# A new order of steps in a fused recurrence and MLP kernel on one core: two more key chunks turned by DMA, fillers placed anew

## The chip, the cores and the metric

The kernel runs on one core of one Trainium2 chip. The metric is the device time of one execution in microseconds (us). The engines of the core are TensorE (PE in the profile, PEld for its weight loads), VectorE (DVE), ScalarE (ACT), GpSimd (POOL) and SyncE (SP). SP computes nothing: it issues DMAs.

## The reference

Two stages, in float32. The first is a linear recurrence with decay over 768 steps, for 4 batches and 8 heads of 48 columns; the second is a normalised MLP with a residual, over the 384 columns of all heads together.

```python
for t in range(S):                                  # S = 768
    cur = u * k_t (outer) v_t
    y[:, :, t] = r_t @ (state + cur)
    state = w[..., None] * state + k_t (outer) v_t
x = y.transpose(0, 2, 1, 3).reshape(B, S, H * D)    # 4 x 768 x 384
xn = (x - mean(x)) / sqrt(var(x) + 1e-6) * g_ln
out = x + relu(xn @ w_ch1) @ w_ch2                  # 384 -> 1536 -> 384
```

## The kernel before

The 768 steps of a batch are cut into 6 chunks of 128 rows, so there are 24 chunks, numbered through all batches. Within a chunk the recurrence is done as masked attention with decay factors multiplied into r and k; from chunk to chunk of a batch a state Z (48 x 48 for each head) is carried. The MLP runs over groups of chunks (`GROUPS`: eight of one chunk, six of two, four of one).

The kernel is a list of small steps, worked out by a planner and written out in the string `PLAN`. A step `NAME,i,e` stands for the function of that name called with number i and engine e (v DVE, s ACT, g POOL, - where the engine is fixed). The steps are issued in the order of the list, and each engine runs its own in that order: a step that waits holds all that is behind it on its engine, and SP's DMAs are held in the same way. The list is what sets the order; nothing is rescheduled later.

The steps, by line of the profile:

- Loads on SP: LK (L344), LR (L349 for two chunks together, L354 for one), LV (L357) bring k, r, v of a chunk; LW1 (L327) a third of the first MLP matrix. IW2 (L341) brings a third of the second matrix on POOL's queue.
- SK and SR (L208) multiply k and r by decay factors; CV (L203, L205) copies v to bf16. The buffers of k, r and v hold 10 chunks.
- Turns: TRK, TRR (L382) turn keys or the queries of two chunks on PE, and TCk, TCr (L203 on ACT, L205 on DVE) copy them out of PSUM. For the chunks of `K_BY_DMA` the keys are turned by DMA instead: TKD (L546) from chunk 12, with the queries still on PE, and TKR (L540) from chunk 14, both together.
- Q (L208) multiplies turned r and k. AT (L414) makes the scores on PE, AM, or AMa and AMb for half of it, (L424) masks them on DVE.
- S (L445, L452, L458) makes the next state and the diagonal term on PE; ZU (L208 or L471) and ZD (L208) update Z; CC (L203, L205) copies the diagonal term; VB (L477) multiplies it with v.
- Y (L487, L495) makes the chunk's output on PE, X (L502) adds VB on DVE, SQ (L509), RS (L523, L526) and XN (L515, L517) normalise.
- The normalised chunk is turned on PE (LT, L555, with copy XT) or by DMA (LT2, L534, for two chunks; LTD, L530).
- UP (L570) is a part of the first matrix product, RL (L586 on ACT, L588 on DVE) its relu, DN (L599) a third of the second product of a chunk. `UP,i` is part i mod 16 of group i div 16, `DN,i` third i mod 4 of chunk i div 4. OT (L657) adds the residual; STO (L664) and STP (L668) store one or two chunks, on ACT's queue (s) or SP's (-). The last chunk goes in halves: DA, DB (L616), OA, OB (L632), SA, SB (L645).
- SW (L334, L338) scales a block of the first matrix; WBM (L298), FK (L302), FR (L306), WL (L320), CT (L231) and CP make factors at the start.
- WU and DU (L281, L285) are matmuls of zeros whose results nobody reads. As long as no DN has been issued a DU,8 is two matmuls of 512 columns into a PSUM tile of its own; afterwards it is eight matmuls of 128 columns into the unread columns of the latest `o` tile.

PSUM has one tile each for `at`, `s`, `y`, `tr` and `o`, and two for `hp`. So the next AT waits for AM, the next Y for X, the next chunk's DN for OT, and so on.

Of the kernel before, what the change touches and what calls it, by code (L numbers as in the profile page):

```python
# [26 lines left out]
SW,3,s X,1,v SW,7,g TRK,3,- S,2,- AM,2,v LV,4,- TCk,3,s XN,1,g UP,0,- CC,2,s SW,8,s LT,1,- VB,2,v Y,2,- SW,6,s
LK,6,- XT,1,v AT,3,- Q,3,v RL,0,s UP,1,- X,2,v SK,4,g CV,3,s UP,17,- ZU,2,v XN,2,s RL,1,v S,3,- SQ,0,s LT,2,-
DU,8,- CC,3,v RL,17,s XT,2,v VB,3,g DU,8,- SQ,2,s TRK,4,- IW2,2,g SR,4,v UP,33,- TCk,4,s SR,5,v RS,0,g UP,34,- RL,33,s
AM,3,v LR,6,- TRR,4,- RS,2,g RL,34,s UP,18,- LV,6,- TCr,4,v Q,4,v DN,0,- RL,18,s ZU,3,v LV,5,- UP,32,- TCr,5,s SK,5,v  # L30
AT,4,- RL,32,s Y,3,- CV,4,g UP,2,- X,3,v TRK,5,- AM,4,v XN,3,g RL,2,s DN,1,- TCk,5,s S,4,- LK,7,- UP,16,- Q,5,v
CC,4,v SK,6,v LT,3,- LK,8,- DN,2,- VB,4,g XT,3,v UP,48,- LR,8,- SR,7,g OT,0,v TRK,6,- ZU,4,v DN,8,- LV,7,- TCk,6,s
SR,6,g Y,4,- RL,16,s LV,10,- DN,9,- X,4,v TRR,6,- XN,4,g DN,10,- TCr,7,v TCr,6,s SK,7,g AT,5,- RL,48,s OT,2,v S,5,-
UP,49,- LK,12,- CC,5,s CV,6,s AM,5,v SQ,1,s DN,4,- LR,10,- CV,5,s TRK,7,- RL,49,v RS,1,g DN,5,- TCk,7,s LK,11,- Q,6,v
AT,6,- SQ,3,s SR,8,v Y,5,- LK,9,- VB,5,v LT,4,- S,6,- XT,4,s SK,8,g UP,50,- X,5,v CC,6,v AM,6,v DN,6,- XN,5,s
LV,8,- Q,7,g CV,7,s UP,64,- LR,12,- RL,50,s OT,1,v Y,6,- SR,9,g SQ,5,s AT,7,- ZU,6,v LV,9,- LT,5,- RL,64,s UP,66,-
XT,5,v VB,6,g AM,7,v CV,10,s LK,10,- TRK,8,- S,7,- TCk,8,s UP,81,- RL,66,s CC,7,v ZU,7,v DN,12,- VB,7,g STO,1,s X,6,v
SQ,4,s TRR,8,- RS,5,g XN,6,v DN,13,- LR,14,- RL,81,s TCr,9,v SK,9,g TCr,8,s UP,82,- LV,12,- Y,7,- RS,3,g LT,6,- LV,15,-
AT,8,- X,7,v XT,6,s DN,14,- Q,8,g SQ,6,s TRK,9,- RL,82,s UP,65,- LR,15,- RS,4,g SR,12,v XN,7,s UP,98,- TCk,9,v RL,65,s
LR,16,- SR,11,g OT,3,v CV,8,s LT,7,- STO,3,s LV,13,- UP,80,- ZD,7,v STO,0,s AM,8,v SR,10,g DN,16,- RL,80,s S,8,- RL,98,s  # L40
SK,10,g DN,17,- XT,7,v LK,13,- CC,8,v ZU,8,v Y,8,- CV,9,g TRR,10,- LK,14,- DN,18,- Q,9,v TCr,11,s SK,11,v AT,9,- TCr,10,s
OT,4,v VB,8,g UP,112,- LV,11,- AM,9,v ZD,8,g TRK,10,- DN,20,- X,8,v S,9,- STO,2,- DN,21,- CC,9,s SK,12,v TCk,10,s Y,9,-
VB,9,g ZU,9,v SQ,8,s TKD,12,- UP,96,- RL,112,s RS,6,g Q,10,v TRK,11,- X,9,v RL,96,s AT,10,- ZD,9,g DN,22,- AM,10,v XN,9,s
UP,113,- XN,8,s SR,14,g TCk,11,s OT,5,v UP,97,- LT2,8,- SR,13,v S,10,- RL,97,s DN,24,- Q,11,v CV,12,s LR,17,- ZU,10,v SK,13,g
AT,11,- CC,10,s CV,11,s RL,113,v DN,25,- LK,15,- VB,10,g AM,11,v S,11,- TKD,13,- TRR,12,- DN,26,- TCr,12,s SR,15,g CC,11,v Y,10,-
SQ,7,s LK,16,- UP,130,- ZD,10,v STO,4,- Q,12,g X,10,v UP,132,- RL,130,s LK,18,- OT,6,v Y,11,- RL,132,s LV,14,- UP,114,- RS,7,g
VB,11,v TCr,13,v DN,28,- X,11,v AT,12,- SK,14,v XN,11,s UP,128,- SR,16,v TKR,14,- RL,114,s AM,12,v S,12,- SQ,10,s DN,29,- SK,15,g
XN,10,s UP,129,- ZU,12,v RL,128,s CV,13,g TKR,15,- DN,30,- RL,129,s Q,13,v Y,12,- SQ,9,s AT,13,- OT,7,v UP,131,- SQ,11,s LT2,10,-
AM,13,v UP,133,- CC,12,s RL,131,s DN,32,- CV,14,s VB,12,v STO,7,- RL,133,s S,13,- LV,17,- AT,14,- CC,13,v X,12,v DN,33,- VB,13,g
LR,18,- ZU,13,v Y,13,- LK,17,- RS,8,g Q,15,v DN,34,- Q,14,v UP,147,- SK,16,g LR,19,- OT,8,v S,14,- AM,14,v RL,147,s DN,36,-  # L50
CV,15,g TKR,16,- UP,144,- RS,9,g ZD,13,v AT,15,- X,13,v RL,144,s UP,146,- CC,14,v ZU,14,v XN,13,s UP,145,- VB,14,v STO,5,s XN,12,v
DN,37,- STO,6,s RL,145,v LT2,12,- SQ,12,s Y,14,- AM,15,v S,15,- RL,146,s DN,38,- SK,18,g LV,16,- UP,148,- OT,9,v LK,21,- SR,17,g
UP,149,- RL,148,s DN,40,- SK,17,v RL,149,s AT,16,- ZD,14,v TKR,17,- DN,41,- X,14,v SR,18,g ZU,15,v UP,160,- CC,15,v Q,16,v LV,18,-
Y,15,- VB,15,g AM,16,v RL,160,s DN,42,- LK,19,- SQ,13,s CV,16,g UP,163,- TKR,18,- OT,10,v CV,17,g UP,165,- RL,163,s ZD,15,v RS,10,g
DN,44,- XN,14,s X,15,v RL,165,s UP,162,- XN,15,v UP,161,- Q,17,v LT2,14,- RL,162,v DN,45,- RL,161,s CV,18,v S,16,- SQ,15,s LV,19,-
DN,46,- SK,19,v LR,21,- AT,17,- Q,18,g OT,11,v UP,164,- ZU,16,v STP,10,- DN,48,- RL,164,s CC,16,v SR,19,v S,17,- STP,8,s ZD,16,g
AM,17,v Y,16,- DN,49,- TKR,19,- UP,181,- VB,16,v DN,50,- X,16,v SR,21,g LR,20,- SQ,16,s AT,18,- LK,20,- UP,177,- OT,12,v CC,17,s
SQ,14,s AM,18,v LV,21,- Y,17,- RL,181,s DN,52,- RL,177,s VB,17,v S,18,- DN,53,- CC,18,s SK,21,g CV,19,s X,17,v UP,178,- VB,18,v
UP,176,- RL,178,s XN,16,v Y,18,- XN,17,v AT,19,- RL,176,s Q,19,v LT2,16,- DN,54,- SR,20,v UP,180,- OT,13,v UP,179,- LR,23,- X,18,v
ZU,18,v TKR,21,- DN,56,- RL,179,s SK,20,v S,19,- RL,180,s XN,18,v DN,57,- CC,19,v SQ,17,s AM,19,v LV,20,- UP,193,- RS,12,g TKR,20,-  # L60
UP,197,- VB,19,v RL,193,s RS,11,g Y,19,- RL,197,s UP,196,- LR,22,- X,19,v DN,58,- XN,19,v RL,196,s LT2,18,- UP,192,- OT,14,v UP,194,-
ZU,19,v RL,192,s CV,20,v LK,22,- DN,60,- SR,23,v RL,194,s STP,12,- Q,20,v AT,20,- ZD,19,g DN,61,- AM,20,v LK,23,- S,20,- DN,62,-
SR,22,g ZU,20,v UP,195,- OT,15,v Q,21,g UP,213,- RL,195,s DN,64,- ZD,20,v RL,213,s CV,21,v Y,20,- CC,20,s SK,22,v DN,65,- VB,20,g
TKR,22,- UP,209,- X,20,v S,21,- SK,23,g DN,66,- RL,209,v XN,20,s UP,208,- CC,21,v LTD,20,- OT,16,v AT,21,- RL,208,s DN,68,- AM,21,v
STP,14,s LV,22,- UP,211,- Q,22,g SQ,20,s LV,23,- DN,69,- RL,211,v TKR,23,- UP,210,- VB,21,v ZU,21,v DN,70,- Y,21,- OT,17,v UP,212,-
CV,22,s RL,210,v DN,72,- RL,212,s X,21,v S,22,- SQ,18,s ZD,21,v DN,73,- CC,22,s ZU,22,v SQ,19,s UP,225,- XN,21,v RS,13,g VB,22,v
DN,74,- LTD,21,- UP,226,- Q,23,g OT,18,v AT,22,- RL,225,v RL,226,s DN,76,- RS,14,g AM,22,v STP,16,s UP,224,- ZD,22,g DN,77,- RL,224,s
Y,22,- SQ,21,s DN,78,- X,22,v RS,15,g S,23,- UP,241,- SQ,22,s OT,19,v XN,22,g AT,23,- CC,23,s DN,80,- CV,23,g AM,23,v LTD,22,-
UP,240,- RS,16,g VB,23,v DN,81,- RL,240,s Y,23,- RL,241,s DN,82,- STP,18,s X,23,v UP,256,- XN,23,s OT,20,v UP,242,- LTD,23,- RL,256,v
# [641 lines left out]
```

## Time and profile before

| | us |
|---|---|
| median of 3 runs | 154.26 (152.65 to 155.15) |
| profiled execution | 153.76 |
| its span, first to last instruction | 151.9 |
| PE busy | 142.9 (94%) |
| DVE busy | 116.9 (77%) |
| ACT busy | 81.1 (53%) |
| POOL busy | 80.6 (53%) |

The page gives busy times of the engines, the span in 40 slices, the DMA queues, a chain of waits followed back from the end, and groups of instructions by line. Matmuls are pipelined, so a busy PE may still be waiting; the starts of its instructions tell more than the busy share. The granted PE clock was full in all slices.

### The profile page before, as it was taken

Reading aid. Unit: us, or ns where it says so; the run is one execution under the profiler, and the core shown is the slowest. Engines: PE = TensorE matmul, PEld = TensorE weight load, DVE = VectorE, ACT = ScalarE, POOL = GpSimd, SP = SyncE. Lnnn points to the kernel's source line nnn. Section 1 sums busy time; section 2 is a strip of 40 time slices with the busy share of each in tenths; the row PEclk is TensorE's granted clock in tenths of the full one; section 3 lists DMA queues with packets and bytes.
Section 4 is the critical chain, followed back from the end, with each engine's and each line's share of the span. In section 5 each row is a group of like instructions: output and inputs, shape, how many; then the busy total and the mean of one; then the engine's idle time right before and its main releaser. Section 6 shows DMA issues by size and latency. Waiting matters only on the chain.

```text
span 151.9 us, 4412 instructions
## 1 busy us (share of the span) xinstructions
PE 142.9 (94%) x1774; PEld 109.3 (72%) x1774; DVE 116.9 (77%) x237; ACT 81.1 (53%) x181; POOL 80.6 (53%) x122
## 2 busy tenths in 40 slices
PE   7999679999999999999999999999998999999991
...
DMA  5999979999999996399989898995995493325021
GB/s 122 229 246 339 340 154 216 224 220 218 223 233 234 190 261 159 84 154 191 184 178 239 182 174 137 309 172 108 193 199 165 94 228 56 129 43 169 0 107 53
DMA packets 90900, 27.16 MB, mean 179 GB/s; under 512 B 86140, under 2 KB 89344, under 8 KB 90880
## 3 DMA queue, kind: packets, MB, share of 16 engines
...
## 4 chain that ended last, share of the span: by engine, by line
PE 64%; DVE 9%; DMA 9%; POOL 6%; issue 4%; ACT 4%; SPq 2%; DVEq 0%; POOLq 0%; ACTq 0%
PE hp L570 24%; PE o L599 22%; DMA vf<-in_v_dram 7%; PE at L414 4%; PE tr L382 3%; PE o L281 3%; DVE A L424 2%; DMA xT<-xn 2%; DVE ot L657 2%; PE y L495 2%; PE s L458 2%; PE y L487 1%; POOL rs L526 1%; ACT sqj L509 1%; PE s L445 1%
## 5 line engine op out<-in xcount | busy, mean ns | idle before, releaser
L570 PE MATMUL hp<-xT,w_sb 128*128 128x128 bf16 (+1 forms) x648 | 57.0, 237 | 0.3 <-DMA xT<-xn 0.3
L599 PE MATMUL o<-w_sb,hT 128*128 128x384 bf16 x276 | 56.0, 326 | 0.7 <-DVE ot L657 0.6
L586 ACT ACTIVATE hT<-hp 128x512 bf16<-128x512 f32 x60 | 35.1, 594 | 34.5 <-PE hp L570 34.0
L570 PEld LDWEIGHTS <-w_sb 128*128 128x128 bf16 x648 | 49.4, 114 | 5.0 <-DMA xT<-xn 0.7
L599 PEld LDWEIGHTS <-hT 128*128 128x128 bf16 x276 | 24.1, 97 | 11.8 <-issue 1.0
L424 DVE TENSOR_TENSOR A<-at,mask 128x1024 bf16<-128x1024 f32 (+1 forms) x26 | 29.3, 1133 | 1.1 <-PE at L414 1.1
L657 DVE SCALAR_TENSOR_TENSOR ot<-o,rs,x 128x384 f32<-128x384 f32 x23 | 14.1, 615 | 9.9 <-PE o L599 6.1
L208 POOL TENSOR_TENSOR sc<-kf,Fk 128x384 bf16<-128x384 f32 x13 | 13.7, 1054 | 13.9 <-PE s L458 8.1
L502 DVE SCALAR_TENSOR_TENSOR x<-y,Vb 128x384 f32<-128x384 f32 x24 | 13.2, 551 | 6.3 <-PE y L495 4.1
L477 POOL TENSOR_TENSOR Vb<-vf,cc 128x384 f32<-128x384 f32 x11 | 9.7, 878 | 13.5 <-DVE cc L205 6.9
L509 ACT ACTIVATE sqj<-x,sm 128x384 bf16<-128x384 f32 x24 | 14.7, 615 | 3.6 <-DVE x L502 2.8
L203 ACT COPY trs<-tr 128x512 bf16<-128x512 bf16 x19 | 11.0, 586 | 10.6 <-PE tr L382 7.1
L281 PE MATMUL o<-warm 128*128 128x512 bf16 x49 | 13.7, 415 | 1.0 <-DVE warm L237 1.0
L523 POOL TENSOR_SCALAR rs<-sq 128x1 f32<-128x1 f32 (+1 forms) x18 | 4.6, 253 | 17.6 <-ACT sqj L509 16.5
L208 POOL TENSOR_TENSOR sc<-rf,Fr 128x384 bf16<-128x384 f32 x12 | 12.7, 1068 | 0.9 <-DMA out_dram<-ot 0.6
L526 POOL TENSOR_TENSOR rs<-rs,expo 128x1 f32<-128x1 f32 (+1 forms) x18 | 12.0, 665 | 1.5
L208 POOL TENSOR_TENSOR q<-trs 128x512 bf16<-128x512 bf16 x8 | 10.3, 1287 | 3.5 <-DMA trs<-sc 3.5
L208 DVE TENSOR_TENSOR sc<-rf,Fr 128x384 bf16<-128x384 f32 x12 | 8.2, 692 | 4.3 <-ACT Fr L306 3.8
L414 PE MATMUL at<-trs 48*128 48x128 bf16 x192 | 9.5, 219 | 1.0 <-ACT trs L203 1.0
L414 PEld LDWEIGHTS <-trs 48*128 48x128 bf16 x192 | 5.5, 94 | 6.2 <-issue 5.2
L382 PE MATMUL tr<-ident,sc 128*128 128x128 bf16 x104 | 8.9, 219 | 0.3 <-DVE trs L205 0.2
L588 DVE TENSOR_SCALAR hT<-hp 128x512 bf16<-128x512 f32 x12 | 8.2, 685 | 0.9 <-PE hp L570 0.9
...
## 6 DMA issues: line engine op xcount, KB each, us to landing
...
```

The lines of the kernel that those rows point to most:

```text
L208: engines[e].tensor_tensor(out=out, in0=in0, in1=in1, op=ALU.mult)
L281: nc.tensor.matmul(out=warm_ps[0][:], lhsT=warm[:], rhs=warm[:].unsqueeze(1).to_broadcast([P, 4, P]), start=True, stop=True)
L382: nc.tensor.transpose(out=t[:, a * HP + q, :], in_=flat[:, q, :], identity=ident[:])
L414: nc.tensor.matmul(out=t[:, par, q, :], lhsT=trs(i)[p0 : p0 + D, 1, q, :], rhs=trs(i)[p0 : p0 + D, 0, q, :], start=True, stop=True,)
L424: nc.vector.tensor_tensor(out=AA(i)[:, a:b].rearrange("p e q t -> p (e q) t"), in0=psum["at", i][:, a:b].rearrange("p e q t -> p (e q) t") ...
L502: nc.vector.scalar_tensor_tensor(out=xx(i)[:], in0=psum["y", i][:, :C], scalar=1.0, in1=Vb(i)[:], op0=ALU.mult, op1=ALU.add, accum_out=sm[ ...
L509: nc.scalar.activation(out=sqj[:], in_=xx(i)[:], func=ACT.Square, bias=sm[i][:], scale=-float(C), accum_out=sq[g][:, j : j + 1])
L526: nc.gpsimd.tensor_tensor(out=rs[g][:], in0=rs[g][:], in1=expo[:, :n], op=ALU.pow)
L570: nc.tensor.matmul(out=t[:, a * gw : (a + 1) * gw].rearrange("p (j t) -> p j t", j=size), lhsT=w1_sb[n][kc][:, fb::FB], rhs=xT(g)[:, :size ...
L586: nc.scalar.activation(out=o, in_=s, func=ACT.Relu)
L599: nc.tensor.matmul(out=psum["o", i][:, :C], lhsT=hT(g)[:, fk, j * P : (j + 1) * P], rhs=w2_sb[d][:, a, :], start=(fk == 0), stop=(fk == FK ...
L657: nc.vector.scalar_tensor_tensor(out=ot(i), in0=psum["o", i][:, :C], scalar=rs[g][:, j : j + 1], in1=xx(i)[:], op0=ALU.mult, op1=ALU.add,)
```

## The change

The list `PLAN` is another one, and the keys of chunks 10 and 11 join `K_BY_DMA`. The functions are the same. Counted over both lists (834 steps each):

| step | before | after |
|---|---|---|
| TRK, TCk | 12 each | 10 each |
| TKD | 2 | 4 |
| DU | 23, all ahead of the first DN | 24 ahead of it, 1 behind DA,2 |
| CC on ACT / DVE | 11 / 13 | 20 / 4 |
| SK on POOL / DVE | 13 / 11 | 16 / 8 |
| SR on POOL / DVE | 12 / 12 | 8 / 16 |
| Q on POOL / DVE | 8 / 16 | 6 / 18 |
| VB on POOL / DVE | 11 / 13 | 14 / 10 |
| XN on ACT / DVE / POOL | 11 / 8 / 5 | 14 / 7 / 3 |
| TCr on ACT / DVE | 8 / 6 | 12 / 2 |
| TCk on ACT / DVE | 11 / 1 | 4 / 6 |
| XT on ACT / DVE | 3 / 5 | 6 / 2 |
| RL on ACT / DVE | 60 / 12 | 61 / 11 |
| CV on ACT / DVE / POOL | 12 / 4 / 8 | 11 / 5 / 8 |
| SW on ACT / POOL | 6 / 3 | 5 / 4 |
| STO and STP on ACT / SP | 11 / 6 | 5 / 12 |

The diff, cut to the set of chunks, the start and the end of the list:

```diff
-K_BY_DMA = [12, 13, 14, 15, 16, 17, 18, 19, 20, 21, 22, 23]
+K_BY_DMA = [10, 11, 12, 13, 14, 15, 16, 17, 18, 19, 20, 21, 22, 23]
...
-MW,0,v WF,0,s MI,0,g LR,0,- MP,0,v DU,8,- LC,0,s LK,0,- TL,0,s MM,0,g DU,8,- LK,2,- WU,13,- LN,0,s LV,0,- LC,1,s
-LV,1,- WBM,0,- DU,8,- LK,1,- FR,1,s DU,8,- FK,0,s SR,0,v DU,8,- LR,2,- FR,2,s SK,0,v DU,8,- FR,0,s SR,1,v TRK,0,-
-LC,2,- DU,8,- SK,2,v TCk,0,s LK,3,- DU,8,- CV,0,s LW1,1,- TRR,0,- DU,8,- LV,2,- TCr,0,s TCr,1,v DU,8,- SK,1,g LW1,0,-
-AT,0,- AMa,0,v LW1,2,- CV,1,g TRK,1,- AMb,0,v LV,3,- CT,0,- DU,8,- Q,0,g CP,0,s TCk,1,s LK,4,- DU,8,- Y,0,- DU,8,-
-UW,0,g Q,1,v AT,1,- SR,2,v TRK,2,- SR,3,g S,0,- TCk,2,s DU,8,- LR,4,- UGC,0,s CC,0,s DU,8,- WL,0,s VB,0,g DU,8,-
-SW,5,s TRR,2,- SW,4,g CV,2,v ZU,0,v SK,3,g X,0,v S,1,- DU,8,- CC,1,v AMa,1,v DU,8,- AMb,1,v DU,8,- SW,0,s SW,1,g
-DU,8,- TCr,3,v TCr,2,s XN,0,g ZU,1,v SW,2,s IW2,1,g AT,2,- VB,1,v LT,0,- Y,1,- Q,2,v IW2,0,g XT,0,s LK,5,- DU,8,-
...
+MW,0,v WF,0,s MI,0,g LV,0,- MP,0,v WU,13,- LC,1,s LK,0,- TL,0,s LK,2,- DU,8,- LR,0,- LN,0,s DU,8,- LC,2,s LK,3,-
+DU,8,- CV,0,g WBM,0,- LK,1,- DU,8,- FK,0,s DU,8,- FR,1,s LV,1,- SK,2,v DU,8,- FR,2,s SK,0,v TRK,2,- DU,8,- LR,2,-
+TCk,2,v DU,8,- SR,1,v TRK,0,- LC,0,- SR,0,v DU,8,- TCk,0,s LW1,1,- DU,8,- LV,2,- TRR,0,- SK,1,g DU,8,- LW1,2,- TCr,0,s
+DU,8,- MM,0,g TCr,1,s LW1,0,- AT,0,- Q,0,v CV,1,s LK,4,- TRK,1,- DU,8,- SR,3,v LK,5,- CT,0,- DU,8,- TCk,1,v CP,0,s
+FR,0,s DU,8,- UW,0,g AMa,0,v WL,0,s AMb,0,v UGC,0,s SR,2,v LV,3,- AT,1,- Q,1,v S,0,- TRR,2,- AMb,1,v CC,0,s SK,3,g
+Y,0,- DU,8,- TCr,2,s AMa,1,v SW,3,s CV,2,g ZU,0,v AT,2,- VB,0,v S,1,- Q,2,v DU,8,- CC,1,s TCr,3,s X,0,v DU,8,-
+SW,5,s ZU,1,v TRK,3,- XN,0,g DU,8,- AM,2,v TCk,3,s VB,1,g Y,1,- SQ,0,s S,2,- SW,6,g LT,0,- SW,8,s X,1,v DU,8,-
+ZU,2,v SW,7,g AT,3,- XT,0,s LR,4,- Y,2,- XN,1,s AM,3,v SW,4,g DU,8,- CC,2,s LK,6,- DU,8,- RS,0,g SW,2,s VB,2,v
+LT,1,- DU,8,- SQ,1,s LV,4,- X,2,v UP,1,- SW,0,g SW,1,s DU,8,- IW2,0,g SK,4,v XT,1,s UP,0,- SK,5,v RL,1,s IW2,1,g
+XN,2,v TRK,4,- RS,1,g RL,0,s UP,17,- LV,5,- TCk,4,v CV,3,s Q,3,v TRK,5,- RL,17,s LR,6,- UP,18,- IW2,2,g TCk,5,v SR,4,v
+LT,2,- S,3,- RL,18,s LK,7,- XT,2,v Y,3,- SR,5,v CC,3,s UP,2,- ZU,3,v SK,6,g TRR,4,- RL,2,s UP,33,- VB,3,v TCr,4,s
+TCr,5,v UP,32,- RL,33,s X,3,v AT,4,- UP,16,- XN,3,v Q,4,v DN,0,- Q,5,v CV,4,v LR,8,- TRK,6,- AM,4,v S,4,- TCk,6,s
...
-RL,258,s RL,272,s DN,90,- STO,21,s UP,274,- OT,22,v DB,0,- STO,22,- RL,274,s DA,0,- DB,1,- DA,1,- DB,2,- DA,2,- OB,23,v OA,23,v
+RL,273,s RL,272,s DN,90,- DB,0,- OT,22,v UP,274,- STO,22,s DA,0,- RL,274,v DB,1,- DA,1,- DB,2,- DA,2,- OB,23,v DU,8,- OA,23,v
 SB,23,s SA,23,-
```

SP's order in the later part, where stores and turns stand among the loads:

```text
before  LK22 STP12 LK23 TKR22 LTD20 LV22 LV23 TKR23 LTD21 LTD22 LTD23 STO22 SA23
after   LK18 LR18 TKR17 LK19 LK22 STP8 LT2,14 TKR18 LK20 LV18 TKR19 LV19 LR20 LV20 LT2,16 STP10 LV21 LR21 LK21
        TKR20 STP12 LT2,18 LK23 LR22 TKR21 LV22 LR23 TKR22 STP14 TKR23 LTD20 LV23 LTD21 LTD22 LTD23 STO21 STP18 SA23
```

More of the change, by code (lines that the diff above doesn't have):

```diff
@@ L27 @@
[L27 to L69, printed above, removed]
@@ new lines @@
+UP,34,- OT,0,v UP,49,- X,4,v CV,5,s VB,5,g LV,6,- DN,8,- RL,34,s RS,2,g XN,4,s UP,50,- SR,7,v SQ,3,s LV,7,- DN,9,-
+SR,6,v SK,7,g RL,50,v LK,10,- LT,4,- Y,5,- XT,4,s DN,10,- RL,49,s SQ,4,s TRR,6,- OT,2,v UP,48,- LV,10,- TCr,7,s SR,9,g
+UP,66,- TCr,6,s LR,15,- SK,8,v DN,4,- RL,66,s X,5,v SR,8,g LK,11,- AT,6,- RL,48,s TRK,7,- AM,6,v CV,6,s DN,5,- CV,7,g
+LK,9,- XN,5,s UP,65,- RS,3,g Q,6,v LV,8,- DN,6,- TCk,7,v RL,65,s Q,7,v S,6,- LR,10,- OT,1,v AT,7,- CC,6,s LT,5,-
+VB,6,g Y,6,- DN,12,- XT,5,v LR,12,- ZU,6,v RS,4,g TRK,8,- X,6,v DN,13,- TCk,8,s AM,7,v S,7,- SQ,5,s TRR,8,- LV,12,-
```

35 lines of the change are left out of this document (34 added, 1 removed).

## The prediction

> **What bounds the kernel now.** I began with the page's first two parts, then laid the step order of PLAN beside TensorE's timeline.
>
> ```profile
> PE 142.9 (94%) x1774; PEld 109.3 (72%) x1774; DVE 116.9 (77%) x237; ACT 81.1 (53%) x181; POOL 80.6 (53%) x122
> ...
> PE   7999679999999999999999999999998999999991
> ...
> DMA  5999979999999996399989898995995493325021
> ```
>
> PE is full but for the first fifth and a few late slices, and the DMA engines are full in the first third. A busy PE may still lose time, so I need step lengths: from one step's first start to the next one's, in the PE timeline (start, us, line; idle time before in brackets).
>
> ```profile
> 20.63 0.36 PE L495 MATMUL y<-vv,A 128*128 128x48 bf16 x8
> 20.84 0.59 PE L281 MATMUL o<-warm 128*128 128x512 bf16 x2
> 21.27 0.39 PE L382 MATMUL tr<-ident,sc 128*128 128x128 bf16 x4
> 21.49 0.24 PE L445 MATMUL s<-uwI,q 128*128 128x2 bf16 x4
> 21.59 0.32 PE L452 MATMUL s<-Z,ident 128*128 128x384 bf16 x1
> 21.75 0.33 PE L458 MATMUL s<-vv,sc 128*128 128x96 bf16 x4
> 21.92 0.83 PE L570 MATMUL hp<-xT,w_sb 128*128 128x128 bf16 x12
> 22.59 0.33 PE L555 MATMUL tr<-ident,xn 128*128 128x128 bf16 x3
> 22.76 0.33 PE L487 MATMUL y<-Z,trs 128*128 128x96 bf16 x4
> 22.93 0.36 PE L495 MATMUL y<-vv,A 128*128 128x48 bf16 x8
> 23.22 0.40 PE L414 MATMUL at<-trs 48*128 48x128 bf16 x8
> 23.55 1.53 PE L570 MATMUL hp<-xT,w_sb 128*128 128x128 bf16 x24
> ```
>
> So Y is 0.38 (22.76 to 22.93, 20.63 to 20.84), an early DU 0.43, TRK 0.22, S 0.43 (0.27 without L452), UP 0.67, LT 0.17, AT 0.33, with some 0.08 more ahead of each AT (22.93 to 23.22 against 20.63 to 20.84). The chain of waits gives two more:
>
> ```profile
> 28.46 0.45 PE tr L382 x8
> ...
> 29.58 0.65 PE o L599 x4
> ```
>
> TRR is 0.45 and DN 0.65. By count: 72 UP at 0.66 (the wide ones stream the same columns) 47.7, 69 DN 44.9, 24 AT 7.9, 24 Y 8.4, 24 S 6.5, TRK, TRR and LT 7.1, six last steps 2.0, 23 DU 9.9, and about 2.9 for WU, WBM and CT: 137.3 us of **PE time** in a span of 151.9. So the order's PE work sets the time, and there remain some 10 us of starts, waits and tail, the only thing that a new order can win. Where they lie:
>
> ```profile
> 9.86 0.40 PE L414 MATMUL at<-trs 48*128 48x128 bf16 x8
> ...
> 16.64 0.24 PE L445 MATMUL s<-uwI,q 128*128 128x2 bf16 x4 [1.21 <-DVE Z L208]
> ...
> 19.95 0.40 PE L414 MATMUL at<-trs 48*128 48x128 bf16 x8 [0.99 <-ACT trs L203]
> ...
> 29.42 0.81 PE L599 MATMUL o<-w_sb,hT 128*128 128x384 bf16 x4
> ...
> 100.52 0.65 PE L599 MATMUL o<-w_sb,hT 128*128 128x384 bf16 x3 [0.34 <-DVE ot L657]
> ...
> 114.64 0.25 PE L445 MATMUL s<-uwI,q 128*128 128x2 bf16 x4 [0.87 <-DVE q L208]
> ...
> 137.53 1.53 PE L570 MATMUL hp<-xT,w_sb 128*128 128x128 bf16 x24 [0.34 <-DMA xT<-xn]
> ...
> 148.01 0.49 PE L616 MATMUL o<-w_sb,hT 128*128 128x192 bf16 x4
> ```
>
> DN,0 starts at 29.42 with 23.8 of PE time ahead of it and 113.5 behind it: 4.6 us lost ahead beside the 1.0 of the start. From 29.42 to PE's end at 148.34 (148.01 and one step of 0.33) are 118.9, so 5.4 are lost behind DN,0; about 1.9 are the 0.08 ahead of the ATs, which stay, and **3.5 are waits**.
>
> **The change part by part.** *Turns by DMA.* TRK,10 and TRK,11 go (2 x 0.22 = 0.44 off PE), with two copies; two turns come onto SP's queue. Times to landing of the two in the trace:
>
> ```profile
> DMA to landing us min/median/max: 2.5/3.6/4.6
> ```
>
> In the new order they are issued 7.4 and 9.1 us of PE time ahead of their first readers, so I cost them at nothing: PE's steps between are the cover, and without it one costs 3.6, at most 4.6, less than either lead.
>
> *Unread matmuls.* 24 early DU instead of 23: +0.43. The 25th stands behind DA,2, the last step, eight 128-column matmuls of 0.67/12 us each: 0.45. It writes unread columns of the accumulator that OA reads. Whether OA waits for it the trace of before cannot show; bounds 0 and 0.45. I take 0.45, as OA is behind it in the order and on one bank. PE time is then 137.3 - 0.44 + 0.43 + 0.45 = 137.7: **no gain in work**.
>
> *Moved work.* DVE gives up nine CC, three SK, three VB, four TCr and takes five TCk, four SR, two Q. From the groups by line (mean ns ahead of the bar's last column):
>
> ```profile
> L477 DVE TENSOR_TENSOR Vb<-vf,cc 128x384 f32<-128x384 f32 x13 | 7.7, 596 | 0.0
> L208 DVE TENSOR_TENSOR q<-trs 128x512 bf16<-128x512 bf16 x16 | 7.7, 489 | 0.4 <-ACT trs L203 0.2
> L208 DVE TENSOR_TENSOR sc<-kf,Fk 128x384 bf16<-128x384 f32 x11 | 7.5, 685 | 0.5 <-PE s L458 0.5
> ...
> L205 DVE COPY trs<-tr 128x512 bf16<-128x512 bf16 x7 | 4.5, 648 | 2.3 <-ACT trs L203 1.5 <-PE tr L382 0.8
> ...
> L205 DVE COPY cc<-s 128x8 f32<-128x8 f32 x13 | 2.1, 159 | 1.2 <-PE s L458 1.1
> ```
>
> With SR at SK's price: -1.4 - 2.1 - 1.8 + 0.65 + 2.7 + 1.0 = -0.9 us. DVE is not heavier, ACT and POOL stand at 53%; load does not decide, positions do.
>
> *The start.* In before S,1 waits for Z, because CV,2 stands ahead of ZU,0 on DVE and waits for its load:
>
> ```profile
> 15.39 0.74 DVE L205 CAST vv<-vf 128x384 bf16<-128x384 f32 x1 [1.81 <-DMA vf<-in_v_dram]
> 16.05 0.54 DVE L208 TENSOR_TENSOR Z<-s,WLZ 128x384 bf16<-128x384 f32 x1
> ...
> 17.35 1.28 DVE L424 TENSOR_TENSOR A<-at,mask 128x512 bf16<-128x512 f32 x2
> ```
>
> CV,2 goes to POOL, but DVE gets the copy of chunk 1's keys. PE's lag at AT,0 is 1.2 (9.86 less the start of 1.0 less 7.7 of PE time); with it TRK,1 ends at about 11.5 in the new order. Behind it on DVE: TCk 0.65, two half masks 1.28, SR 0.55, Q 0.42, two half masks 1.28, Z 0.54, in all 4.7, so S,1 at about 16.3 instead of 16.64. From S,1 to DN,0 the new order has 13.5 of PE time (11.1 in before: it brings real work forward). AT,2, which waited 0.99 for TCr,2 behind TCr,3 and a weight scaling, now stands ahead of S,1; its copy comes first. On this stretch I add 0.2 for two ATs and 0.5 for chunk 4's queries:
>
> ```profile
> 26.93 1.02 DVE L208 TENSOR_TENSOR sc<-rf,Fr 128x384 bf16<-128x384 f32 x2 [0.50 <-DMA rf<-in_r_dram]
> ...
> 15.86 3.75 SPq L349 DMA_DIRECT2D rf<-in_r_dram  x1
> ```
>
> LR,4, issued at 15.86, landed only near 26.9. The new order puts LK,5 ahead of it, but issues the second matrix's loads (19.0 in before, row below) behind SW,0, which follows RS,0 and so SQ,0 on ACT: at about 22.6, an estimate from the orders and the page's durations. So LR,4 meets less of them. SR,4 can start at 25.3 by DVE's order. Bounds: no wait (LR,4 at 25), or 2.7 (at 28.0, 26.9 and one load more). I take 0.5, nearer to the first, as the competing loads start later. Those loads then land in time for DN,0:
>
> ```profile
> L341 POOL DMA_DIRECT2D w_sb<-in_moe_w_ch_dram x3: 543/607/786, 19.0 to 27.0; - x3
> ...
> DMA to landing us min/median/max: 5.5/6.3/6.8
> ```
>
> that is 28.1 to 29.4. **DN,0 at 16.3 + 13.5 + 0.7 = 30.5**, with 111.2 left: 141.7, against 29.42 + 113.5 = 142.9. **Gain 1.2**, the last DU paid.
>
> *Behind DN,0.* I set, for every ring of one or two PSUM tiles and each chain such as Y, X, XN, turn, UP, the PE time between releasing and waiting step against the durations: none of either order is too short by more than 0.1 us, so the 3.5 come from engines that run late. Of the largest, LV,22 no longer stands behind two waiting turns and LTD,22 has 3.7 of PE time to its UP instead of 2.3; LTD,20 is tighter (2.4 instead of 6.2). I keep 2.5 of the 3.5: **gain 1.0**, bounds 3.0 (only 0.5 stays) and a loss of 3.3 (below).
>
> Sum: 153.76 (the profiled execution, 1.9 above its span) - 2.2 = 151.6; against the median 154.26 it is **152.1 us**, and I forecast on that scale. A measurement of this kernel tells about 2% from no change, 3.1 us.
>
> **Rivals.** *A, the waits nearly all go:* LR,4 in time and no AT late gains 1.9 ahead of DN,0, 3.0 behind: 154.26 - 4.9 = 149.4. For it: all slacks are positive. Against: before's are too, and it still lost 8 us.
>
> *B, SP's line holds the loads.* SP takes six more stores and two turns. STP,8, waiting for OT,9, now stands ahead of LT2,14, TKR,18, LK,20 and LV,18; CV,18 on ACT needs LV,18 3.6 of PE time after its issue. Rows of before for such a hold (SP waits, then ACT waits):
>
> ```profile
> SPq L540 <- DVE sc L208: 5.5, 4, 3.4
> ...
> ACT vv L203 <- DMA vf<-in_v_dram: 3.3, 1, 3.3
> ```
>
> It decides once DVE runs more than STP,8's lead of 4.9 us late; then XN,16, RL,179 and S,18 queue behind CV,18. One hold of 3.3 on PE with before's late waits kept: 154.26 - 1.2 + 3.3 = 156.4, slower; two make 159.7. Against it: the other stores stand 3.6 us and more behind their OT. The Trainium skill, page "DMA: Bandwidth & Descriptors", section "Anatomy of one DMA — SWDGE (gpsimd) path", says that DMA engines never wait on semaphores and the issuing sequencer does, which speaks against a store on SP; the trace's waits of SP agree.
>
> *C, the early loads stay the bound:* LR,4 lands at 28.0, DVE stands 2.7 at SR,4, TRR,4 and all behind follow, DN,0 at 32.7: 0.8 to 1.0 lost there, 1.0 gained later: 154.2, no change. For it: DMA slices of 9 until 60 us. That the change does nothing is part of this case.
>
> **How the numbers follow.** Forecast 0.45 (own range 150.7 to 153.5), A 0.22, B 0.15, C 0.18. Range 149.3 to 156.8: it takes in A, C and one hold of B, and leaves out two holds. Faster by over 2% (below 151.2): A and a quarter of the forecast, 0.33. Slower by over 2% (above 157.3): two holds or one of C on top, 0.13. Within 2%: 0.54.
>
> **What would show it.** S,1 near 16.3 and its wait for Z gone; DN,0 at 30 to 31; the wait before L208's first two-row group of chunk 4 below 1 us; PE's last step 0.45 longer; behind DN,0 about 2.5 us of waits, none above 1. Wrong if DN,0 is past 31.7, if ACT waits 3 us for a value load, or if the waits behind DN,0 are above 4 us in sum.

## The result, and the profile after

The changed kernel took 153.11 us (median of 20 runs, 150.43 to 155.49), the kernel before 154.20 us on the same chip (20 runs, 152.65 to 156.85). The ratio is 0.986 with a 95% interval of 0.982 to 0.990: faster by 1.4%, clear of no change, but by less than 2%. Every ratio here leaves out the executions that ran over 1.5% longer than the fastest of their kernel, which are 12 of these 20 of the changed kernel, its first profiled one among them; the medians of all 20 give 0.993. Two further measurements gave 0.984 (0.979 to 0.989) and 0.986 (0.981 to 0.990). The rows below are from the second profile of the changed kernel, an execution of 152.21 us; the first, of 153.54 us, and the third, of 150.77 us, are used for the scatter.

The page of the changed kernel:

```profile
span 150.4 us, 4424 instructions
...
PE 143.3 (95%) x1776; PEld 109.6 (73%) x1776; DVE 114.4 (76%) x225; ACT 81.9 (54%) x192; POOL 78.8 (52%) x121
...
PE   7999999999999999999998999999999998999991
...
DMA  5999999999979988999999898996998964312321
```

TensorE's share rose by a point because the span shrank, not its work. The first fifth of its row is filled, and the DMA engines, which had a gap in slices 16 and 17 before (6 and 3), now stand at 6 or more until slice 33, but for the first.

TensorE's timeline of the changed kernel, at the places that the prediction named (start, us, line; idle time before in brackets):

```profile
16.14 0.24 PE L445 MATMUL s<-uwI,q 128*128 128x2 bf16 x4
...
22.47 0.59 PE L281 MATMUL o<-warm 128*128 128x512 bf16 x2
23.43 0.86 PE L570 MATMUL hp<-xT,w_sb 128*128 128x128 bf16 x12 [0.37 <-POOL w_sb L338]
...
30.50 0.81 PE L599 MATMUL o<-w_sb,hT 128*128 128x384 bf16 x4
...
32.22 0.81 PE L599 MATMUL o<-w_sb,hT 128*128 128x384 bf16 x4 [0.25 <-DMA w_sb<-in_moe_w_ch_dram]
...
34.30 0.81 PE L599 MATMUL o<-w_sb,hT 128*128 128x384 bf16 x4 [0.22 <-DMA w_sb<-in_moe_w_ch_dram]
...
67.94 0.23 PE L414 MATMUL at<-trs 48*128 48x128 bf16 x2 [0.46 <-DMA trs<-sc]
...
127.06 0.86 PE L570 MATMUL hp<-xT,w_sb 128*128 128x128 bf16 x12 [0.51 <-DMA xT<-xn]
...
146.46 0.61 PE L291 MATMUL o<-warm 128*128 128x128 bf16 x8
```

S,1 (16.14) no longer waits, and DN,0 starts at 30.50. With the 111.2 us of PE time left, that makes 141.7 against 142.9 before: a gain of 1.2. The last step, the unread DU, begins at 146.46 and takes 0.45, so PE ends at 146.9, and 146.9 - 30.50 - 111.2 = 5.2 us are lost behind DN,0, against 5.4. In the third profile DN,0 starts at 30.31 and 4.0 are lost, in the first 31.01 and 6.0. So the start is steadier, and what lies behind it moves by 2 us from one execution to the next. Of the kernel before there is one profile only, so the parts of the gain are known no better than that. All the waits with a bracket here, but the one at 23.43, end with the landing of a DMA.

TensorE's waits by cause in the changed kernel (line, released by: us in total, times, longest):

```profile
PE o L599 <- DVE ot L657: 0.6, 1, 0.6
PE hp L570 <- DMA xT<-xn: 0.5, 1, 0.5
PE o L599 <- DMA w_sb<-in_moe_w_ch_dram: 0.5, 2, 0.2
PE at L414 <- DMA trs<-sc: 0.5, 1, 0.5
PE hp L570 <- POOL w_sb L338: 0.4, 1, 0.4
```

and the same view of the kernel before:

```profile
PE s L445 <- DVE Z L208: 1.4, 2, 1.2
PE at L414 <- ACT trs L203: 1.0, 1, 1.0
...
PE s L445 <- DVE q L208: 0.9, 1, 0.9
PE o L599 <- DVE ot L657: 0.6, 2, 0.3
PE hp L570 <- DMA xT<-xn: 0.3, 1, 0.3
```

In this profile the order took away 3.3 us of waits for DVE and ACT (the first three rows of before) and brought 1.2 of waits for transfers more (1.5 against 0.3), and 0.4 for a weight scaling on POOL. Not every wait for an engine is gone: in the third profile AT,1 waits 0.8 us for a mask on DVE.

### The profile page after: what moved, and what is told of

Its sections match the earlier page's. It is cut to its first block, busy times and chain, and to the rows that moved or that the text cites. A ratio compares the mean times of both kernels' runs of the same rounds, so it can differ in the third digit from the quotient of the medians.

```text
span 151.8 us, 4424 instructions
## 1 busy us (share of the span) xinstructions
PE 143.4 (94%) x1776; PEld 109.8 (72%) x1776; DVE 114.0 (75%) x225; ACT 81.9 (54%) x192; POOL 78.7 (52%) x121
## 4 chain that ended last, share of the span: by engine, by line
PE 55%; DMA 19%; POOL 11%; issue 5%; SPq 5%; DVE 2%; ACT 1%; POOLq 0%; DVEq 0%
PE hp L570 22%; PE o L599 21%; DMA trs<-sc 7%; DMA w_sb<-in_moe_w_ch_dram 6%; DMA rf<-in_r_dram 3%; PE at L414 3%; SPq L344 3%; DMA xT<-xn 3%; POOL w_sb L338 2%; PE y L495 2%; POOL sc L208 2%; POOL Vb L477 2%; PE s L458 2%; PE tr L382 1%; PE y L487 1%
## 5 line engine op out<-in xcount | busy, mean ns | idle before, releaser
L586 ACT ACTIVATE hT<-hp 128x512 bf16<-128x512 f32 x61 | 35.7, 596 | 38.7 <-PE hp L570 38.6
L208 POOL TENSOR_TENSOR sc<-kf,Fk 128x384 bf16<-128x384 f32 x16 | 16.5, 1031 | 17.0 <-DMA kf<-in_k_dram 10.0
L657 DVE SCALAR_TENSOR_TENSOR ot<-o,rs,x 128x384 f32<-128x384 f32 x23 | 14.1, 615 | 10.1 <-PE o L599 7.2
L477 POOL TENSOR_TENSOR Vb<-vf,cc 128x384 f32<-128x384 f32 x14 | 12.0, 854 | 18.8 <-ACT cc L203 10.9
L281 PE MATMUL o<-warm 128*128 128x512 bf16 x51 | 15.6, 431 | 1.0 <-DVE warm L237 1.0
L203 ACT COPY trs<-tr 128x512 bf16<-128x512 bf16 x16 | 9.1, 588 | 8.3 <-PE tr L382 5.9
L208 DVE TENSOR_TENSOR q<-trs 128x512 bf16<-128x512 bf16 x18 | 10.5, 586 | 3.1 <-ACT trs L203 1.7
L208 POOL TENSOR_TENSOR q<-trs 128x512 bf16<-128x512 bf16 x6 | 7.2, 1196 | 5.9 <-PE hp L570 5.9
L515 ACT ACTIVATE xn<-x,sm 128x384 bf16<-128x384 f32 x14 | 8.6, 617 | 2.3 <-DVE x L502 2.3
L208 POOL TENSOR_TENSOR sc<-rf,Fr 128x384 bf16<-128x384 f32 x8 | 8.3, 1042 | 1.3 <-PE tr L382 1.3
L208 DVE TENSOR_TENSOR sc<-kf,Fk 128x384 bf16<-128x384 f32 x8 | 5.4, 695 | 4.7 <-ACT Fk L302 4.7
```

The lines of the kernel that those rows point to most:

```text
L208: engines[e].tensor_tensor(out=out, in0=in0, in1=in1, op=ALU.mult)
L281: nc.tensor.matmul(out=warm_ps[0][:], lhsT=warm[:], rhs=warm[:].unsqueeze(1).to_broadcast([P, 4, P]), start=True, stop=True)
L477: engines[e].tensor_tensor(out=Vb(i)[:].rearrange("p (h d) -> p h d", h=H), in0=vf(i)[:], in1=cc(i)[:].unsqueeze(2).to_broadcast([P, H, D] ...
L586: nc.scalar.activation(out=o, in_=s, func=ACT.Relu)
L657: nc.vector.scalar_tensor_tensor(out=ot(i), in0=psum["o", i][:, :C], scalar=rs[g][:, j : j + 1], in1=xx(i)[:], op0=ALU.mult, op1=ALU.add,)
```

## The experiments

My theory, from here on: the new order gains by removing the waits for engines, and gives part of that back to transfers (the second matrix's thirds, LTD,20) and to the last DU. Each kernel below is the changed one with one edit, unless said otherwise. Ratios are to the kernel before on the same chip.

**The changed kernel again, and a third time.**

> The changed kernel itself, beside the three others of this call on one chip, so that differences from it need not go over another chip. Every theory: about 1% below the kernel before (153.1 against 154.2 us).

> The changed kernel once more, as the yardstick for the three kernels beside it on the same chip. Both theories: 1.4 to 1.6% below before, so about 151.9 us where before is 154.1, with TensorE's waits at DN,1, DN,2 and UP,224 in its timeline again and 5 to 6 us lost behind DN,0.

Measured: 151.77 us (6 runs), ratio 0.9836 (0.9787 to 0.9885), and 151.53 us (6 runs), ratio 0.9857 (0.9814 to 0.9899). In the third profile nothing shows a wait for the second matrix any more, while UP,224 and AT,12 still wait for theirs. Its loss behind DN,0 is 1.2 us smaller (4.0 against 5.2), and the two waits at DN,1 and DN,2 are about 0.8 of that (by their steps, that is from one step's start to the next one's, less the PE time between).

**The last unread matmul taken away.**

```diff
-OB,23,v DU,8,- OA,23,v
+OB,23,v OA,23,v
```

> The changed order without its last step of unread matmuls (DU behind DA,2). Theory (OA waits for them, as its start at 148.46 and the DU's end at 148.42 in the trace suggest): OA starts right behind OB, the tail is 0.4 to 0.45 us shorter, about 152.7. Rival (the two happen to end together, OA is held by OB alone): no difference, 153.1.

Measured: 151.20 us (6 runs), ratio 0.9826 (0.9787 to 0.9865). The end of DVE's timeline, first of the changed kernel, then of this one (whose line numbers are 11 lower):

```profile
146.34 0.42 DVE L632 SCALAR_TENSOR_TENSOR ot<-hp,rs,x 128x192 f32<-128x192 f32 x1 [0.60 <-PE hp L616]
147.11 0.42 DVE L632 SCALAR_TENSOR_TENSOR ot<-o,rs,x 128x192 f32<-128x192 f32 x1 [0.36 <-PE o L291]
```

```profile
145.09 0.42 DVE L621 SCALAR_TENSOR_TENSOR ot<-hp,rs,x 128x192 f32<-128x192 f32 x1 [0.60 <-PE hp L605]
145.42 0.41 DVE L621 SCALAR_TENSOR_TENSOR ot<-o,rs,x 128x192 f32<-128x192 f32 x1
```

From OB's start to OA's it is 0.77 with the DU and 0.33 without: OA does wait for the unread matmul, and it costs 0.44 at the end. The times point the same way (0.57 between the medians), but their intervals overlap; the trace settles it.

**The second matrix's first two thirds loaded earlier.**

```diff
-S,2,- SW,6,g
+S,2,- IW2,0,g IW2,1,g SW,6,g
...
-DU,8,- IW2,0,g SK,4,v
+DU,8,- SK,4,v
...
-RL,1,s IW2,1,g XN,2,v
+RL,1,s XN,2,v
```

> The changed order with IW2,0 and IW2,1 (loads of the second matrix, on POOL's queue) moved ahead of SW,6, some 4.5 us earlier. Theory (the waits of 0.7 and 0.2 us ahead of DN,1 and DN,2 in the trace are for these loads, which landed at 31.0 and 33.1): the loads land near 27, both waits vanish, DN,2 starts about 1.2 us earlier, time 1.2 below the changed kernel. Rival (the DMA engines are full there, so LK,4 to LK,6 and LR,4 land later by what these loads land earlier): SR,4 and TRR,4 late by 1 us or more, no gain or a loss of up to 1 us.

Measured: 153.16 us (12 runs), ratio 0.996 (0.9933 to 0.9988), 1.3% slower than the changed kernel beside it (0.996 / 0.9836). The loads landed, and DN,1 and DN,2 waited no more; but POOL's timeline, TensorE's waits, and the timelines of DVE and TensorE (the line numbers are 11 lower) show the price:

```profile
18.41 1.34 POOL L330 DMA_DIRECT2D w_sb<-in_moe_w_ch_dram  x2
19.80 2.34 POOL L327 TENSOR_SCALAR w_sb<-w_f,g_neg 128x512 bf16<-128x512 f32 x3
...
PE hp L559 <- POOL w_sb L327: 1.6, 2, 1.0
...
28.27 0.56 DVE L197 TENSOR_TENSOR sc<-rf,Fr 128x384 bf16<-128x384 f32 x1 [1.35 <-DMA rf<-in_r_dram]
...
29.15 0.87 PE L371 MATMUL tr<-ident,sc 128*128 128x128 bf16 x8 [0.36 <-DVE xT L194]
```

Issuing the two loads holds POOL for 1.34 us, the scaled weights SW come that much later, and the first UPs wait 1.6 instead of 0.4. That part the rival did not name. Its own part came too, at a smaller price: SR,4 waits 1.35 us for its load of r, the copy XT,2 behind it on DVE is late, and TRR,4 waits 0.36 for that. DN,0 slips by 1.8 to 32.32, for 0.8 us of waits saved at DN,1 and DN,2: the rival's time was right, its reason in part.

**The two halves of the new order alone.** One kernel has the new order up to DN,2 and the old rest; the other the old order up to the steps around DN,1 and the new rest, with the few steps that the seam needs in between.

```diff
 new start: RL,32,s S,5,- AM,5,v RL,16,s      (new list up to here)
+UP,34,- RS,2,g RL,34,s LV,6,- DN,2,- ...     (then the old list)
 new rest:  TRK,5,- AM,4,v XN,3,g RL,2,s      (old list up to here)
+... X,4,v CV,5,s VB,5,g DN,8,- XN,4,s UP,50,-  (then the new list)
```

> The steps of the new order up to DN,2 of chunk 0, then the remaining steps in the old order (keys of chunks 10 and 11 on PE, no unread matmuls at the end). Theory (the gain is made at the start: less PE time left behind DN,0): 0.7 to 1.5 us below the kernel before, about 153.0. Rival (the start is equal, the gain lies in the later order): equal to before, 154.2.

> The steps of the old order up to DN,1 of chunk 0, then the remaining steps in the new order (keys of chunks 10 and 11 by DMA, unread matmuls at the end). The other mixture, new start and old rest, was 1.1% slower than the kernel before. Theory (the later order is what gains; start and rest meet at a seam that costs up to 1 us): faster than before by 0.5 to 1.5%, waits behind DN,0 near 4.5 us. Rival (neither half gains alone; buffers, loads and PE order of one half fit only its own other half): slower than before by about 1%, waits behind DN,0 of 7 us as in the other mixture.

Measured: 155.42 us, ratio 1.011 (1.007 to 1.015), and 155.98 us (6 runs), ratio 1.013 (1.007 to 1.018). Neither half gains alone; both are slower than before. The profile kept of the second is of an execution of 169.19 us at a granted clock of 0.85, so its loss behind DN,0 can't be set against the 4.5 or 7 us that were expected. In the first, DN,0 stands at 31.05, which with 111.2 left makes 142.3, a gain of 0.6 kept, and then the old rest brings its old waits in TensorE's timeline:

```profile
100.87 0.81 PE L588 MATMUL o<-w_sb,hT 128*128 128x384 bf16 x4 [0.43 <-DVE ot L646]
114.99 0.25 PE L434 MATMUL s<-uwI,q 128*128 128x2 bf16 x4 [0.87 <-DVE q L197]
```

These are the two waits that the prediction quoted of before at 100.52 and 114.64. Waits at the seam and at UP,256 come on top: 7.2 us are lost behind DN,0. So these two waits come with the old rest. What the seam itself costs can't be parted from what the half is worth, so the sizes of the halves stay open.

Where the waits belong is clearer from all profiles together, those of the experiments below included. S,1's wait for Z and AT,2's for its copy are in both profiles with the old start (1.21 and 0.99 in before, 0.40 and 0.71 in the kernel with old start and new rest) and in none of the twelve with the new one. Eleven of these twelve have UP,0's wait for SW,0 instead (0.37 us at least, with longer waits in some), and five have one of 0.3 to 0.9 us at AT,1 for a mask.

**Keys of chunks 10 and 11 on TensorE again.** Both leave `K_BY_DMA`.

```diff
-SK,11,g TKD,10,- LT,6,-      -RL,80,s TKD,11,- DN,18,-
+SK,11,g LT,6,-               +RL,80,s DN,18,-
+TCr,11,v TRK,10,- TCk,10,s XN,8,s
+UP,97,- TRK,11,- TCk,11,s X,9,v
```

> The changed order with the keys of chunks 10 and 11 turned on PE again: TRK,10 and TCk,10 behind TCr,11, TRK,11 and TCk,11 behind UP,97, no TKD,10 and TKD,11. Theory (the two turns by DMA are covered, they take 0.44 us off PE and nothing else): 0.45 us slower than the changed kernel, up to 0.9 with the copies on ACT. Rival (TKD,10 and TKD,11 hold SP by 2.6 us and make LK,13 and TKD,12 late, for which AT,12 waits 0.6 to 1.1): the wait at AT,12 goes, 0.2 to 0.7 us faster than the changed kernel.

Measured: 152.56 us (12 runs), ratio 0.9935 (0.9903 to 0.9966). TensorE's timeline has a new wait:

```profile
59.19 0.40 PE L382 MATMUL tr<-ident,sc 128*128 128x128 bf16 x4 [0.38 <-DVE trs L205]
```

TRK,10 waits for the one `tr` tile, which TCr,11 has just emptied; by its step it loses 0.54. With the 0.44 of the two TRK that is 1.0 us, and AT,12's wait of 0.5 to 0.7 goes. This kernel is 0.7 to 1.0% above the changed one, 1.1 to 1.5 us, so 0.7 to 1.1 of it has no row. The rival falls: the kernel isn't faster. That AT,12 does not wait here is no sign that TKD,10 and TKD,11 make it wait, for it does not wait in any of the seven profiles of the other experiments that keep both turns in the changed order, either; one of them, without the last DU, has the changed order up to its end. That the two turns by DMA are worth more than their TensorE time, because they also free the tile, is argued from the one wait of TRK,10 and not shown; the site I chose for TRK,10 is part of the price.

**Every store on the queue that it had before.**

```diff
-STO,0,-   STO,1,-   STO,3,-   STO,6,-   STP,8,-   STP,14,-   STO,21,-   STP,18,-   STO,7,s   STO,22,s
+STO,0,s   STO,1,s   STO,3,s   STO,6,s   STP,8,s   STP,14,s   STO,21,s   STP,18,s   STO,7,-   STO,22,-
```

> The changed order with every store on the queue that it had before (11 on ACT, 6 on SP, instead of 5 and 12). Theory (stores on SP stand early enough behind their OT that they hold nothing): same time as the changed kernel within 0.4 us. Rival (SP's line is held by them, STP,8 before LV,18 and STP,14 before TKR,23 and LTD,20): waits at AT,17 and UP,224 shrink by 0.3 us and more each, 0.5 to 1.5 us faster.

Measured: 150.14 us (6 runs), ratio 0.9814 (0.9763 to 0.9866): 0.2 to 0.5% below the changed kernel, within the intervals. SP's waits in the changed kernel and its timeline show why it is so little:

```profile
SPq L664 <- DVE ot L657: 3.1, 1, 3.1
...
SPq L668 <- DVE q L208: 2.0, 1, 2.0
...
88.79 2.02 SPq L668 DMA_DIRECT2D out_dram<-ot  x1
...
140.68 0.36 SPq L664 DMA_DIRECT2D out_dram<-ot  x1
```

The 3.1 us are the hold of STO,21 just ahead of 140.68, behind which SP has only STP,18 and SA,23, both stores. The 2.0 us are STP,8's, which does stand ahead of loads and turns; in the third profile it took 0.7. No wait of ACT for a value load, which was 3.3 us before, is left in the changed kernel. UP,224's wait, which the rival has shrink, is 0.8 with the old queues against 0.5 and 0.7. The traces differ more (3.4 us lost behind DN,0, no wait for a second-matrix third), but those thirds are issued long before the first store, so their landing in time is chance.

**Three repairs in one.** No last DU; RS,0 on POOL behind IW2,1, so that SW,0 and the loads come sooner; VB,21 behind XN,20.

```diff
-RS,0,g SW,2,s ... SW,0,g SW,1,s DU,8,- IW2,0,g ... IW2,1,g XN,2,v
+SW,2,s ... SW,0,g SW,1,s DU,8,- IW2,0,g ... IW2,1,g RS,0,g XN,2,v
-VB,21,g UP,211,- OT,17,v XN,20,g AT,22,-
+UP,211,- OT,17,v XN,20,g VB,21,g AT,22,-
-OB,23,v DU,8,- OA,23,v
+OB,23,v OA,23,v
```

> The changed order without the last step of unread matmuls; RS,0 on POOL moved from ahead of SW,0 to behind IW2,1; VB,21 moved behind XN,20. Theory: UP,0's wait of 0.5 us for SW,0 goes, the second matrix lands 1.2 us earlier and the waits ahead of DN,1 and DN,2 (0.4 and 0.3) go, OA starts 0.44 earlier, UP,224 waits 0.3 less: 1.5 us below the changed kernel, 2.5% below before. Rival (as with IW2 far ahead: earlier loads of the second matrix make LR,4 late, SR,4 and TRR,4 wait): only the end's 0.4 us remains.

Measured: 153.34 us (6 runs, 149.94 to 154.38), ratio 0.9821 (0.9747 to 0.9896, from two of the six): no better than the changed kernel's, within the interval. The profile kept is of the first run, 153.97 us, which the ratio leaves out; what the two runs of 149.94 and 151.57 us did has no row. In the kept profile UP,0 waits no more, and DN,0 starts at 30.04: the repair of SW,0 did what it was to do. POOL issues the loads at 21.60 instead of 23.32, and a value load is late on DVE, and TensorE behind it:

```profile
33.62 0.36 DVE L205 CAST vv<-vf 128x384 bf16<-128x384 f32 x1 [2.90 <-DMA vf<-in_v_dram]
```

```profile
34.03 0.48 PE L458 MATMUL s<-vv,sc 128*128 128x96 bf16 x4 [2.69 <-DVE vv L205]
```

That the earlier issue made this load late is not shown. The load is LV,4. In the changed kernel itself the next one, LV,5, took 5.3 us to landing in the second profile and 11.1 and 10.1 in the first and third, so such loads take that long at times without the edit; LV,5 is needed later, and nothing waited for it. What the stretch is like is in the windows of the changed kernel (us; busy time of each engine; granted clock; DMA share; GB/s):

```profile
22.00:26.00 4.00, 3.63 (x60) 3.14 (x58) 3.41 (x9) 2.87 (x6) 3.74 (x7) 1.00 1.07 217
26.00:30.00 4.00, 4.00 (x82) 3.74 (x80) 3.52 (x8) 2.44 (x5) 1.52 (x2) 1.00 1.03 201
```

A share of 1.0 and more: all sixteen DMA engines are busy. That a load which goes earlier pushes back another fits the late load of r with the second matrix moved 5 us earlier, and is argued here.

**Fewer early fillers.** The last three DU ahead of UP,0 left out (their results are unread).

```diff
-LK,6,- DU,8,- RS,0,g ... LT,1,- DU,8,- SQ,1,s ... SW,1,s DU,8,- IW2,0,g
+LK,6,- RS,0,g ... LT,1,- SQ,1,s ... SW,1,s IW2,0,g
```

> The changed kernel with 21 of its 24 early unread matmul pairs: the last three ahead of UP,0 are left out. Theory (TensorE waits there for the scaled weights of SW,0 anyway, and the fillers only fill that wait): UP,0 starts where it did, with an idle stretch of up to 1.8 us ahead of it, and the time stays within 0.3 us. Rival 1 (they stand on the path): DN,0 1.3 us earlier, 0.8% faster. Rival 2 (an idle TensorE is granted a lower clock afterwards): the granted clock in the slices behind 22 us falls below full and the time is longer.

Measured: 151.14 us (6 runs), ratio 0.983 (0.9794 to 0.9867), 0.3% below the changed kernel, within the intervals. TensorE's timeline and two stretches:

```profile
23.96 0.86 PE L570 MATMUL hp<-xT,w_sb 128*128 128x128 bf16 x12 [1.92 <-POOL w_sb L338]
```

```profile
22.00:24.00 2.00, 0.08 (x2) 0.04 (x2) 2.00 (x5) 1.39 (x3) 1.91 (x3) 1.00 1.10 262
24.00:26.00 2.00, 2.00 (x36) 2.00 (x37) 0.89 (x4) 1.14 (x3) 1.83 (x4) 1.00 1.08 203
```

TensorE stands idle for 1.92 us, of which the three fillers had covered 1.3, and UP,0 starts no sooner (23.96 against 23.43): the scaled weights of SW,0 set it. Both rivals fall: the 0.8% does not come, and the granted clock stays at 1.00. A unit of PE time ahead of UP,0 is not a unit of time.

**The last DU out and the old queues of the stores; then UP,224 one step later.** The first kernel joins the two edits shown; the second adds:

```diff
-S,23,- UP,224,- OT,18,v ... LTD,21,- DN,76,- CC,22,v
+S,23,- OT,18,v ... LTD,21,- DN,76,- UP,224,- CC,22,v
```

> The changed kernel without the unread matmul behind DA,2 and with each store on the queue it had before. Theory (the tail is 0.4 us longer for the unread matmul, and the stores on SP cost a little through late turns): 0.4 to 0.9 us below the changed kernel, 151.0 to 151.5 at a yardstick of 151.9, and OA directly behind OB. Rival (both are hidden, and what the single edits showed was chance): equal to the changed kernel within 0.3 us.

> The kernel b_two with UP,224 moved behind DN,76, so that 0.65 us of TensorE work more stands between the turn by DMA LTD,20 and its first reader. Theory (the wait ahead of UP,224 is for the turn alone): it falls from 0.6 to 1.3 us to 0 to 0.6, and the time is 0.5 us below b_two. Rival (what follows needs UP,224 and its relu in time, or DN,76 itself waits for its relu): the wait shows at DN,76 or UP,225 instead, and the time equals b_two.

Measured: the first 0.9785 (0.9736 to 0.9833, from three of six runs that spread from 150.14 to 155.22 us), against 0.9857 of the changed kernel beside it; the second **149.99 us** (6 runs, 149.59 to 150.84), ratio **0.976 (0.972 to 0.980)**. That is 1.0% below the changed kernel, with intervals that don't meet, and the best of all. What UP,224 alone is worth (0.9759 against 0.9785) is within the intervals. TensorE's timeline of the first and of the second:

```profile
125.42 0.86 PE L570 MATMUL hp<-xT,w_sb 128*128 128x128 bf16 x12 [0.83 <-DMA xT<-xn]
```

```profile
125.26 0.24 PE L445 MATMUL s<-uwI,q 128*128 128x2 bf16 x4 [0.31 <-ACT cc L203]
...
125.64 0.81 PE L599 MATMUL o<-w_sb,hT 128*128 128x384 bf16 x4
126.29 0.83 PE L570 MATMUL hp<-xT,w_sb 128*128 128x128 bf16 x12
```

The wait for LTD,20 (0.97 by the step, 0.83 in the bracket) is gone; S,22, which now follows S,23 at once, waits 0.45 by its step for CC: half of it moved, though not to DN,76 or UP,225 as the rival had it, and half was saved. UP,224 waits for LTD,20 in all ten profiles with the changed order at this place, by 0.4 to 1.2 us, and does not in this second kernel's.

## Why the prediction was right, and where its steps were not

The forecast on the scale of 154.26 was 152.1, a ratio of 0.986, and the measured one is 0.986: the likeliest case came, at its size. That it agrees to the last digit is luck, as one execution differs from the next by more than the gain (profiled ones took 153.54, 152.21 and 150.77 us where 151.6 was forecast), and as some of the terms below were wrong. Step by step:

- *No gain in work, the last DU at 0.45.* Right: 0.44 by OB and OA. The bound 0 is excluded.
- *DVE lighter by 0.9, load doesn't decide.* DVE lost 2.5 (116.9 to 114.4): the sum left out three XT, one XN and one RL that go from DVE, and one CV that comes. It did not decide, as TensorE's waits show.
- *S,1 at 16.3.* 16.14, the wait for Z gone. Right.
- *DN,0 at 30.5, gain 1.2.* 30.50 and 30.31; right in sum, by two errors that cancel. **The 0.5 for LR,4 failed:** in the second profile nobody waited for a load of r, though these landed much later than before (median 8.2 against 4.5 us; in the first profile DVE waited 0.3):

```profile
L349 SPq DMA_DIRECT2D rf<-in_r_dram x7: 629/705/6243, 2.6 to 44.9; - x7
...
who waited for it (us, times):
busy tenths in 40 slices 0000000000000000000000000000000000000000
DMA to landing us min/median/max: 4.5/8.2/12.6
```

  The list of those who waited for it is empty. In its place UP,0 started 0.53 late (22.47 + 0.43 = 22.90, against 23.43): it needs SW,0, which follows RS,0 on POOL. I had used that very chain to place the second matrix's loads, and not asked what TensorE needs from SW,0. The LR,4 term has its place where the second matrix is loaded earlier: there SR,4 did wait 1.35.
- ***"Those loads then land in time for DN,0" failed.*** By line, in the changed kernel:

```profile
L341 POOL DMA_DIRECT2D w_sb<-in_moe_w_ch_dram x3: 546/608/906, 23.3 to 25.7; - x3
...
  PE o L599: 0.5, 2
...
DMA to landing us min/median/max: 6.7/7.9/8.6
```

  I took one issue time, 22.6, for all three and before's 5.5 to 6.8 us to landing. They were issued from 23.3 to 25.7 and took 6.7 to 8.6, so the first third came in time for DN,0, and the others late for DN,1 and DN,2 by 0.4 each. The margin had been 1.1 us, and the change puts more loads into the same stretch. The Trainium skill, page "DMA: Bandwidth & Descriptors", section "Anatomy of one DMA — SWDGE (gpsimd) path", fits such a load as 2.0 us and its bytes at 436 GB/s, which for 384 KB makes an estimate of 2.9 us. The trace disagrees: here such loads took 6.7 to 8.6 us, in a stretch in which the DMA share was 1.0 and more.
- *Waits behind DN,0 2.5 of 3.5 kept, none above 1: gain 1.0.* The gain was 0.2 and 1.4 in the second and third profiles and a loss of 0.6 in the first, so the size is within what one execution can show, and 1.0 is not confirmed. Less the 1.9 that it set aside for the ATs, the sum of the waits was 3.3, 2.1 and 4.1, where 2.5 was expected and 4 was to be the sign of being wrong. The 1.9 counts all 24 ATs; 20 of them stand behind DN,0 in before, 1.6 us, so the 3.5 was 3.8. "None above 1" held in the second and third profiles and failed in the first, where UP,224 waited 1.35 by its step; in all profiles of the changed kernel it is the largest wait behind DN,0 or close to it. The prediction had read LTD,20 as "tighter" and given it no price: 2.4 us of PE time against the 2.3 to 3.3 us that these turns (L530) took to landing in before was a wait of up to 0.9 to write down. AT,12's wait for TKD,12 (0.5 to 1.0 in the three profiles) was missed too. The two turns added were costed by their own readers' leads, not by the turn that stands behind them on SP; whether they make that turn late is not shown.
- *Rival B.* It did not come. STP,8 held SP for 2.0 us and 0.7 in two profiles, and ACT waited for no value load. Putting the stores back gave 0.2 to 0.5%, within the intervals.
- *Rival C.* DN,0 was not late for LR,4. Its mechanism, full DMA engines in the early stretch, fits the late thirds at DN,1 and DN,2 and, in the kernel that loads the second matrix earlier, the late load of r; the larger part of that kernel's loss was POOL's time to issue the loads.
- *Rival A, 149.4.* It did not come for the changed kernel. The last kernel nearly reached it (149.99), with the last DU, the stores and UP,224 mended.

What stays open: how the gain parts between the halves of the list, what the stores alone cost, why the keys of chunks 10 and 11 on TensorE cost 0.7 to 1.1 us more than their rows, and what makes the loss behind DN,0 move by 2 us between executions.
